# Agent attention and a SoLU layer on one core: the written-out order of five queues replaced by another

## The chip, the core and the metric

The kernel runs on one core of a Trainium2 chip. The metric is the device time of one execution in microseconds (us), as the median of several runs. Engines are called PE (TensorE matrix products; PEld its weight loads), DVE (VectorE), ACT (ScalarE), POOL (GpSimd) and SP (SyncE, which issues the DMAs here).

## What is computed

Four batches of 12,608 tokens with 128 channels, 49 agents per batch; the attention's output goes through a layer of 1,024 hidden units whose activation is a SoLU with a layer norm.

```python
a2k = sm(agents, k)                 # softmax(scale * agents @ k.T)
agent_v = a2k @ v
x = sm(q, agents) @ agent_v         # then reshaped to (50432, 128)
h = x @ w_in
solu = h * softmax(h)
ln = (solu - mean) / sqrt(var + 1e-06) * g_ln
out = ln @ w_out
```

## The kernel before

**Tiles.** The 50,432 tokens are 394 tiles of 128. All steps of all tiles are built as operations (class Op: an engine, a function, the operations it depends on) and issued in an order that a table gives.

**Phase A**, once per batch (`phase_a`, lines 562 to 825): 13 chunks of K and V come in by DMA (`kload` L580, `vload` L586 and L591), PE makes the agents' scores (L597), DVE their maxima, ACT the exponentials, PE turns them (L630) and multiplies with V (L650). At the end agent_v is multiplied with w_in, and the product stands in SBUF as two fp16 matrices, `mh` and `ml`. For batch 0 this is the head of the program; for the other batches it is spread over the tiles of the batch before.

**Phase B**, once per unit of 8 tiles (`phase_b`): queries come in by DMA (`qload` L840), PE makes logits (L858), DVE, ACT and POOL make exp and pack it as fp16 pairs (`pack`), a DMA transpose (L888) writes it turned to `pT` (a ring of 3), and PE sums it (L901) for the row's scale.

**Each tile x** then takes these steps:

- H (`c_h`, L950, PE): four products of 512 columns of pT with mh and ml into `ph`, a PSUM tile of 1,024 columns; there are two, `ph` of even and of odd tiles. H of x needs U of x-2.
- MX (`c_max`, L966, DVE): scaled copy of ph to `e` with its row extreme.
- EX (`c_exp`, L973, ACT): exp into ph, with its sum.
- U (`c_u`, L981, DVE): the product `u` (ring of 6), with its sum.
- SQ (`c_sq`, L1002, ACT): sum of squares.
- For 343 of the tiles: F0 (`c_f0`, L989 on POOL or L987 on ACT) rounds u to fp16 into `f` (ring of 5), F1 (`c_f1`, L992, POOL) writes the remainder beside it, XT (`c_x`, L996, SP) is a DMA transpose of both into `x` (ring of 8, x_a to x_h), and W (`c_w`, L1030, PE) multiplies it with w_out: 24 products of 128 columns, in four parts of six, between which other work may stand.
- For the other 51 tiles: PE turns u (`c_t`, L1009), ACT or DVE copies it (L1014), and W is 8 products in fp32.
- Four tiles share a PSUM tile `px` for their W. FIN (`c_fin`, L1077, DVE) scales the four by one over the standard deviation, and OUT (`c_out`, L1081) writes 256 KB to HBM. There are four `px`, which phases A and B use too.

**The order.** `STEPS` (lines 25 to 148) is a compressed table; `steps()` unpacks it to pairs of an operation's number and a choice of engine (F0, copies and small casts have two). `Plan.run` issues the operations in that order:

```python
        todo = steps()
        for i, k in todo:
            o = self.ops[i]
            e = o.eng[k]
            assert o.left == 0
```

So the table sets the order of instructions on each engine and of the transfers on SP's queue. Each engine works through its own in order and waits where data isn't there; no time of the plan is imposed. The model times that `Plan.run` keeps choose the `px` tile of an operation and the number of idle products that PE makes in the head (`idle`, L1088, of `ones`). At the end every instruction is tied to the one before on its engine, so nothing is moved later.

Of the kernel before, what the change touches and what calls it, by code (L numbers as in the profile page):

```python
# [25 lines left out]
    "c-pOb4^%5{THoX)aJejUZsTm6r7XQ7W%Fgz$cG#b%TkJIj44t?M8p`gk#Z0zMH;i&ER7tbkwaseBC<$Rj1kj_h=|C^i7}f^DN>}EL(^=&EagxR"  # L26
    "Vmii%91b6s8<Ls6Gm}3v3Ex@k>4lpxGw-~Ap7(ivzu)t`E&P)np-{NFVtSYm+VPdv>(=DZb?a7AaetXqY%4CuFE*FmC-MN0g_bwo+&A3%mBc2x"
    "Hy;`twfV+xSJiJ+ohYiPvCrHpeQU!F_jt$cy=i6L0PZ5X(-=BG|8`%P?5go-MplANg2jo3+x@wfNUdi3*tXHDn4UD&Yid>>CU&%7{ri6x>)<yz"
    "dNkG!+oR3_Y_r<X@!MYK$jWe|tG~v)bakMeHl4KZYp2IM?~dA0r+@aM_Z*#aAJs_1jnxUq*;Z5n0`h^CX_K&aK(q*eVJQuI{b>WfnXZ^1&V^`9"
    "2JlcF7LgxSV+m;lS2@~a0$Bp*ON2JPO|d(6EB2odW7sc!M@lOiM;H8?B5ec<Nh4qwiv%WzCsqe!n8FqTperdEys7(-A0!0}jTjal#(eS>XUrl)"  # L30
    "hvIe_7U(;|TmWb{?CAqR?51K8fBx=3LU-JD^w4YoldGaSbZfzl1JIqqcEu{pf!z;nv`X>KH&r(Zq19>-w}zsaI?-jG*dAZGz7_WzV?7vQiSic>"
    "8xd>GgBq77C2nw1s|jA1&>#4$W^Goq5%l4=qNwjoE5|KSp{u4g7@5{8eR}(YS+yC_@3qDcB;tBGoR%}Zgf@o<By0MxTc&l%T~nY!W2!+h;7Wwt"
    "YK!sb%R~L=b(q(^Xa(Zf7e4McYf>%fRsH?NUDMk$*ITtf|8`h>ej;pmBRIct=@UXJHneGMu4<Ct(M1%@{IB10X)I2(wMDxZl|=WFy)rB!jvbHU"
    "k%Now1Gh|SRLX!eD8;oBR4^`=Yxj1sj^iDp*0eKL)4bAsXSeLsb~G!5Nw8=&Y}M}Hm<WMn?1#VRJ?t7aMCKw<o9X)Ze>OVWxqOXvG>1XE9*Azy"
    "*jn<+^Cl(~yN4IsEgKz|jgEy4tPur^2jik!JUrLaCzCaA;$Dqtff)8n{7B_c)#a3FL8j{)Xl$vjBeoZ9P4z-Beh|}p0&=4Tbu?@Vc1<o!xY%SD"
    "4s1uJ6H(|asMgkWu)Xqg<Vp+=>9zaI+Of&5ElE_QyHii!;+}*-h@Ru!0Br6DQU^|DcmeQ<!xSzd<RAQ+S8HvSMWq{x?(Lz<Gh8MfTMx*$aP6>L"
    "@admkn=mzm8yy`xiTF<ZNIk+|f2z7@pI){atikkJLvQz}qfP2C&yGxt*Gj79=XPb55!-!Y$MD@>)_6{^w_~m2gFp2nmx7@I)B4!Oh*g3M>zpIb"
    "glG2=Pqw2V<s84PzUXYZu6c;mygf>YsvN4S`t9K;Mo6}YL(PH5nNhh47{o1p%-L6?{gp4CPtA01h0d(a!tJ3YM+8?WTJ9$CVPKxsRapGOu;iOR"
    "w=C7U7Y(+g1-E$m_hRC}*#fWy_k%J;C=dan(d!DAIB_eMeBp~D_>yKw?FB)Zd$^%<6djxs$A%-qsK+3Uw0ODz;M=C7H8WZ>4zR=)u2D4`-}pLi"
    "!Xw_E)4Iuh_h2P(0i^war~-ZaL(b~)p20u)8sYl$PmfpH$F&=ZISi`@V7dZWG;@FT0bx^0vFPc|ttHtX`tk3QYW%%ZE8r3{pEmF}WuByS_MiTN"  # L40
    "e|x&kuEr)--2F8b*KdKOeol%HpR^?FbV*a&PQ6{-9cZu*JXZI9^koaNG=;>5qjgTjMzc?UI5uN^`kn7-K!tkeLHCLhjr+rn4JAN?5tpIKv;fwH"
    "{K{G}I_l`DP!0Fb-^SJ9ctk05T4K>Bbr2IPrB-xeZ4>iYWkG#wNa?{1KKc1XP#BenV>45~_=QEK5fh^TDDH=K0q3I$2Gg0^QGwao=XzAT1H0$G"
    "sjWm;vrj!b;~5#+uJSe3R&CVzahc}vxV{|#tKlm@1GYyUqmFx(XXI}_99;(1*{g=f>bVt<X?6gw9Wgbcy93SPm3VJL1RRz%*{yid;Hs13?X4l("
    "{rn}~iGKK_Cw<cPKm6g?LAR{g9TSA7qwewESuw5y;H`OfV)4yA_@f_tux`YiOW*f3H&W-`@C6qi!RF<zRq51&@hhS9(pc}(AU@HyxaYnjaOSGA"
    "6E_PNhPVzGhhwV9&62NryDl9QsMI5v<eR^&@iyO1fqm_!%BI(-eKuD@ba1V41peOFu&Bu94frK$ARg$(lk2_c#*zRy1ARj4qNHchIqJCB(}!&C"
# [36 lines left out]
    "8pIPVap)D-fBLywv}(8Bv6RN{tA)3BPYr+l3(nx+&10e~Sknr+BifCi(5nYqO?6l2(nY00yfPIN2b?Yx%*q1dFRlINf!ZAi5lUj)Y*QQvh7Kmc"
# [1193 lines left out]
```

## Time and profile before

| | us |
|---|---|
| median of 3 runs (lowest, highest) | 1345.69 (1345.56, 1348.81) |
| the profiled execution, own time | 1351.38 |
| its span, first to last instruction | 1349.6 |
| mean granted TensorE clock | 0.980 |

How to read it: the rows further below come from one profiled execution. An engine's idle time stands beside the instruction that came after it, with what ended the wait. A DMA's row on SP is the time that SP took to issue it; its landing is told apart. Matmuls overlap, so the times of single rows on PE do not add up; the start of one to the start of the next does.

### The profile page before, as it was taken

How to read it: one execution, taken by the hardware profiler on the slowest of the kernel's cores; microseconds unless marked ns; L12 is line 12 of the kernel's file. 1: busy time of each engine (PE TensorE's matmuls, PEld its weight loads, DVE VectorE, ACT ScalarE, POOL GpSimd, SP SyncE). 2: the span in 40 equal slices, each digit the busy share in tenths (PEclk: the TensorE clock that was granted, in tenths of full speed). 3: DMA queues.
4: the chain of work that ended last, by engine and by line, in shares of the span. 5: the costliest groups of instructions: out<-in, count | busy, mean ns of one | idle time of the engine just before them, and what ended most of it. 6: DMA issues, size and time to landing. Idle time of an engine off the chain costs nothing.

```text
span 1349.6 us, 36468 instructions
## 1 busy us (share of the span) xinstructions
PE 1215.8 (90%) x14321; PEld 921.6 (68%) x14321; DVE 1179.0 (87%) x2124; ACT 1177.3 (87%) x2151; POOL 1133.5 (84%) x919
## 2 busy tenths in 40 slices
PE   8888898999998898988998888989999989999997
PEld 4666576777776676766767666766777767777676
DVE  6788797989998887988989888988899989999996
ACT  5579797988998987978989788988889989999997
POOL 3488697888997887887988889898789989999995
PEclk9899999999999999989999999999899999999999
DMA  9699999999999999999999999999998999999997
GB/s 375 181 211 221 240 214 245 234 234 185 216 235 232 231 237 229 201 241 225 216 210 216 220 240 228 246 239 244 227 192 177 231 216 211 213 208 224 193 194 176
DMA packets 805484, 300.62 MB, mean 223 GB/s; under 512 B 770496, under 2 KB 774080, under 8 KB 805312
## 3 DMA queue, kind: packets, MB, share of 16 engines
q1 hardware_dynamic: 805312, 298.30, 105.3%
q8 instruction: 112, 1.84, 0.6%
q14 instruction: 60, 0.49, 0.1%
HBM read 79.67 MB, written 25.82 MB: 78 GB/s over the span
## 4 chain that ended last, share of the span: by engine, by line
POOL 22%; DMA 19%; ACT 16%; PE 15%; issue 15%; DVE 12%; SPq 1%; POOLq 0%; DVEq 0%; ACTq 0%
ACT ph L973 7%; ACT sq L1002 6%; PE px L1030 6%; PE ph L950 4%; DVE e_b L966 3%; POOL f_a L992 3%; POOL f_d L992 3%; POOL f_b L992 2%; POOL f_e L992 2%; POOL f_c L992 2%; DVE e_a L966 2%; POOL f_e L989 2%; POOL f_b L989 1%; DMA x_a<-f_c 1%; POOL f_d L989 1%
## 5 line engine op out<-in xcount | busy, mean ns | idle before, releaser
L973 ACT ACTIVATE ph<-e_a,nm 128x1024 f32<-128x1024 f32 x197 | 219.0, 1112 | 74.6 <-DVE e_a L966 73.7
L973 ACT ACTIVATE ph<-e_b,nm 128x1024 f32<-128x1024 f32 x197 | 219.0, 1112 | 23.5 <-DVE e_b L966 22.4
L950 PE MATMUL ph<-mh,pT_a 128*128 128x512 f16 x264 | 101.5, 384 | 8.1 <-DVE u_a L981 4.4
L950 PE MATMUL ph<-mh,pT_b 128*128 128x512 f16 x260 | 99.4, 382 | 9.8 <-DVE u_c L981 3.7
L950 PE MATMUL ph<-mh,pT_c 128*128 128x512 f16 x260 | 99.7, 384 | 4.3 <-DVE u_a L981 1.2
L950 PE MATMUL ph<-ml,pT_a 128*128 128x512 f16 x264 | 101.5, 384 | 0.0
L950 PE MATMUL ph<-ml,pT_c 128*128 128x512 f16 x260 | 99.7, 384 | 0.0
L950 PE MATMUL ph<-ml,pT_b 128*128 128x512 f16 x260 | 99.2, 381 | 0.0
L1030 PE MATMUL px<-wh,x_f 128*128 128x128 f16 x688 | 75.6, 224 | 17.0 <-DMA x_f<-f_b 5.2
L966 DVE TENSOR_SCALAR_CACHE_REDUCE e_a<-ph,nk_a 128x1024 f32<-128x1024 f32 x49 | 62.6, 1278 | 29.4 <-PE ph L950 29.0
L1030 PE MATMUL px<-wh,x_g 128*128 128x128 f16 x688 | 75.2, 225 | 13.6 <-DMA x_g<-f_d 4.3
L981 DVE SCALAR_TENSOR_TENSOR u_a<-e_a,cb,ph 128x1024 f32<-128x1024 f32 x66 | 84.1, 1275 | 3.4 <-ACT ph L973 2.5
L1030 PEld LDWEIGHTS <-x_f 128*128 128x128 f16 x1032 | 65.5, 101 | 31.0 <-DMA x_f<-f_b 6.0
L981 DVE SCALAR_TENSOR_TENSOR u_d<-e_b,cb,ph 128x1024 f32<-128x1024 f32 x66 | 84.2, 1276 | 2.1 <-ACT ph L973 1.5
L981 DVE SCALAR_TENSOR_TENSOR u_c<-e_a,cb,ph 128x1024 f32<-128x1024 f32 x65 | 82.9, 1276 | 3.2 <-ACT ph L973 2.6
L981 DVE SCALAR_TENSOR_TENSOR u_b<-e_b,cb,ph 128x1024 f32<-128x1024 f32 x65 | 82.9, 1275 | 2.4 <-ACT ph L973 2.2
L981 DVE SCALAR_TENSOR_TENSOR u_e<-e_a,cb,ph 128x1024 f32<-128x1024 f32 x65 | 82.9, 1275 | 2.0 <-ACT ph L973 1.5
L981 DVE SCALAR_TENSOR_TENSOR u_f<-e_b,cb,ph 128x1024 f32<-128x1024 f32 x65 | 82.9, 1276 | 1.6 <-ACT ph L973 1.1
L1030 PEld LDWEIGHTS <-x_g 128*128 128x128 f16 x1032 | 65.2, 101 | 27.6 <-DMA x_g<-f_e 5.6
L1030 PE MATMUL px<-wh,x_d 128*128 128x128 f16 x688 | 73.4, 221 | 10.9 <-DMA x_d<-f_e 4.4
L950 PEld LDWEIGHTS <-pT_b 128*128 128x128 f16 x520 | 47.1, 98 | 50.3 <-issue 20.9
L1030 PE MATMUL px<-wh,x_b 128*128 128x128 f16 x688 | 73.5, 221 | 7.3 <-DMA x_b<-f_e 3.7
(473 smaller groups left out, 4811.2 us busy)
## 6 DMA issues: line engine op xcount, KB each, us to landing
out_dram<-ob_a SPq DMA_DIRECT2D x49, 256.0 KB, 3.6
out_dram<-ob_b SPq DMA_DIRECT2D x49, 256.0 KB, 2.8
qt_a<-in_qT_dram SPq DMA_DIRECT2D x24, 512.0 KB, 4.7
qt_b<-in_qT_dram SPq DMA_DIRECT2D x24, 512.0 KB, 4.8
kt_a<-in_kT_dram SPq DMA_DIRECT2D x18, 512.0 KB, 5.0
kt_b<-in_kT_dram SPq DMA_DIRECT2D x18, 512.0 KB, 5.1
vt_b<-in_v_dram SPq DMA_DIRECT2D x18, 512.0 KB, 5.1
vt_a<-in_v_dram SPq DMA_DIRECT2D x18, 512.0 KB, 5.0
```

What stands on the lines that cost most here:

```text
L950: nc.tensor.matmul(ph[:, sl], w, m[:, sl], start=(q == 0), stop=(q == len(mm) - 1))
L966: nc.vector.tensor_scalar(out=nhs[x], in0=phs[x], scalar1=nkr[k % 4][:, j : j + 1], scalar2=None, op0=ALU.mult, op1=ALU.min, accum_out=nms[x])
L973: nc.scalar.activation(out=phs[x], in_=nhs[x], func=AF.Exp, scale=-1.0, bias=nms[x], accum_out=rs_[R]["S"][:, j : j + 1])
L981: nc.vector.scalar_tensor_tensor(out=u, in0=nhs[x], scalar=scal(x)[:, 4:5], in1=phs[x], op0=ALU.mult, op1=ALU.mult, accum_out=su)
L989: nc.gpsimd.tensor_scalar(out=f[:, 0, :], in0=us[x][0], scalar1=1.0, scalar2=0.0, op0=ALU.mult, op1=ALU.add)
L992: nc.gpsimd.tensor_tensor(out=fs[x][:, 1, :], in0=us[x][0], in1=fs[x][:, 0, :], op=ALU.subtract)
L1002: nc.scalar.activation(out=sq, in_=u, func=AF.Square, bias=su, scale=-float(DF), accum_out=rs_[R]["Q"][:, j : j + 1])
L1030: nc.tensor.matmul(po, ut, wt[:, kf, :], start=(q == 0), stop=(q == len(mm) - 1))
```

## The change

`STEPS` holds other numbers, and the table is one line longer, so that every line behind it counts one more (L1030 is now L1031). No other line differs: the same 6,893 operations, tiles, ring sizes and transfers, and the same code. The order was planned anew, with a reserve between the landing of each transfer and the use of its data; the planner is not part of the file.

```diff
 STEPS = (
-    "c-pOb4^%5{THoX)aJejUZsTm6r7XQ7W%Fgz$cG#b%TkJIj44t?M8p`gk#Z0zMH;i&ER7tbkwaseBC<$Rj1kj_h=|C^i7}f^DN>}EL(^=&EagxR"
...
+    "c-pOb4^V1tdf(v{y<9%y7<$T_&vmS^#!!|J<G99J$8}xGu!dU48p2xE5Mmi)EaMu+5^AlnhOmTK;~K|WYKbw_u+|u3T-UI~_!&d2>l%jevDO%C"
...
 )
```

The same place on PE in both orders, the second-layer product of tile 135, whose transposed data stand in x_g (x_f is tile 134, t_b tile 136; ph_167 is H of an odd tile, ph_166 of an even one). Before:

```order
L950 MATMUL ph_167<-mh_4346,pT_a 128x512
...
L1009 MATMUL px_169<-ident,u_e 128x128 x4
L1030 MATMUL px_171<-wh_93,x_f 128x128
...
L1030 MATMUL px_171<-wh_93,x_g 128x128
...
L858 MATMUL px_169<-ag_sb,qt_a 64x49 x16
L1030 MATMUL px_168<-w_92,t_b 128x128 x2
L950 MATMUL ph_166<-mh_4346,pT_a 128x512
```

The first row is H of tile 141, the last H of tile 142. Now:

```order
L951 MATMUL ph_166<-mh_4319,pT_a 128x512
...
L631 MATMUL px_169<-ident,ek_b 128x128 x4
...
L951 MATMUL ph_167<-mh_4319,pT_a 128x512
...
L1031 MATMUL px_170<-wh_93,x_g 128x128
...
L651 MATMUL px_169<-vt_a,eT_a 64x128 x8
...
L1031 MATMUL px_168<-w_92,t_b 128x128 x6
```

Here the first rows are H of tile 142 and the first half of H of 143: the first product of tile 135 stood behind H of 141 and stands now behind H of 142 and half of 143. Over all 343 transposed tiles, the last tile whose H has begun ahead of W of tile x is x + 6.5 in the mean before and x + 7.3 now; x + 5 or less for 49 of them before and for 8 now.

The queue of SP around the transpose of tile 135 (x_g<-f_d), before:

```order
L996 DMA_TRANSPOSE x_e<-f_b 128x16x128
L996 DMA_TRANSPOSE x_f<-f_c 128x16x128
L586 DMA vt_b<-in_v_dram 128x1024
L840 DMA qt_b<-in_qT_dram 128x1024
L1081 DMA out_dram<-ob_a 128x512
L996 DMA_TRANSPOSE x_g<-f_d 128x16x128
L888 DMA_TRANSPOSE pT_c<-pack_a 128x8x128
L1081 DMA out_dram<-ob_b 128x512
L580 DMA kt_a<-in_kT_dram 128x1024
L996 DMA_TRANSPOSE x_h<-f_e 128x16x128
```

Now:

```order
L997 DMA_TRANSPOSE x_e<-f_b 128x16x128
L581 DMA kt_a<-in_kT_dram 128x1024
L841 DMA qt_b<-in_qT_dram 128x1024
L997 DMA_TRANSPOSE x_f<-f_c 128x16x128
L1082 DMA out_dram<-ob_b 128x512
L1082 DMA out_dram<-ob_a 128x512
L997 DMA_TRANSPOSE x_g<-f_d 128x16x128
L581 DMA kt_b<-in_kT_dram 128x1024
L587 DMA vt_b<-in_v_dram 128x1024
L889 DMA_TRANSPOSE pT_c<-pack_a 128x8x128
L997 DMA_TRANSPOSE x_h<-f_e 128x16x128
```

Before, two loads and a store stand ahead of x_g; now two loads stand ahead of x_f and two stores ahead of x_g. Over the queue from its 60th transfer on, a load of K, V or Q stands directly behind another one 29 times before and 48 times now, and three in a row 6 times before and 13 now.

PE's end, from the last H (ph_167 of tile 393) on. Before:

```order
L950 MATMUL ph_167<-mh_13491,pT_a 128x512
...
L1030 MATMUL px_168<-wh_93,x_e 128x128
...
L1009 MATMUL px_170<-ident,u_c 128x128 x4
L1009 MATMUL px_171<-ident,u_c 128x128 x4
```

Now:

```order
L951 MATMUL ph_167<-mh_13536,pT_a 128x512
...
L1031 MATMUL px_168<-wh_93,x_c 128x128
...
L1031 MATMUL px_171<-wh_93,x_d 128x128
...
L1031 MATMUL px_171<-wh_93,x_e 128x128
...
L1010 MATMUL px_170<-ident,u_c 128x128 x4
```

Between the last H and the turn of tile 392 (u_c) stood the W of x_d from its middle and that of x_e and part of x_f; now a quarter of x_b, and the W of x_c, x_d and x_e, which is 1.75 tiles' W more behind the last H in all.

## Rows read from the trace of the kernel before

**Rows 1.** Page, part 1: busy time, share of the span, instructions of each engine.

```profile
PE 1215.8 (90%) x14321; PEld 921.6 (68%) x14321; DVE 1179.0 (87%) x2124; ACT 1177.3 (87%) x2151; POOL 1133.5 (84%) x919
```

**Rows 2.** Waits: who <- for whom: us in total, times, longest.

```profile
ACT ph L973 <- DVE e_a L966: 73.7, 63, 6.9
DVE e_a L966 <- PE ph L950: 59.0, 44, 6.3
```

**Rows 3.** Line L996, the transposes: who waited (us, times); time from issue to landing.

```profile
  PE px L1030: 72.3, 63
...
DMA to landing us min/median/max: 3.6/4.6/9.9
```

**Rows 4.** Timeline of SP near 520 us: start, time to issue, line, transfer.

```profile
519.99 0.54 SPq L586 DMA_DIRECT2D vt_b<-in_v_dram  x1
520.59 0.45 SPq L840 DMA_DIRECT2D qt_b<-in_qT_dram  x1
...
521.63 5.57 SPq L996 DMA_TRANSPOSE x_g<-f_d  x1
527.62 1.26 SPq L888 DMA_TRANSPOSE pT_c<-pack_a  x1
```

**Rows 5.** Timeline of PE there: start, us; in brackets the idle time before.

```profile
531.59 0.29 PE L1030 MATMUL px<-wh,x_g 128*128 128x128 f16 x1 [4.32 <-DMA x_g<-f_d]
```

**Rows 6.** Who waited for L996 in six windows from 100, 400, 500, 600, 800 and 900 us (us, times).

```profile
  PE px L1030: 10.0, 10
  PE px L1030: 11.4, 10
  PE px L1030: 11.0, 6
  PE px L1030: 1.0, 1
  PE px L1030: 4.8, 5
  PE px L1030: 2.9, 4
```

**Rows 7.** The six windows: length, busy us (instructions) by engine, PEclk, DMA share, GB/s.

```profile
100.00:200.00 100.00, 87.54 (x1031) 64.19 (x1029) 85.93 (x152) 85.55 (x157) 80.35 (x63) 1.00 1.16 227
400.00:500.00 100.00, 89.68 (x1040) 67.04 (x1039) 86.71 (x151) 87.40 (x162) 83.52 (x66) 0.98 1.11 236
500.00:600.00 100.00, 88.85 (x1001) 67.48 (x1000) 82.54 (x146) 83.48 (x155) 79.38 (x63) 0.95 1.09 225
600.00:700.00 100.00, 91.86 (x1137) 71.58 (x1136) 88.32 (x164) 89.49 (x168) 85.59 (x69) 0.98 1.10 223
800.00:900.00 100.00, 91.84 (x1106) 69.06 (x1104) 90.11 (x162) 89.80 (x166) 87.22 (x65) 1.00 1.13 236
900.00:1000.00 100.00, 88.16 (x1050) 67.76 (x1048) 85.20 (x155) 86.24 (x163) 84.81 (x68) 0.97 1.13 237
```

**Rows 8.** Waits of PE: four pairs of tiles with their longest wait last.

```profile
PE px L1030 <- DMA x_a<-f_c: 5.7, 3, 4.0
...
PE px L1030 <- DMA x_b<-f_e: 3.7, 1, 3.7
...
PE px L1030 <- DMA x_f<-f_a: 4.7, 3, 3.3
...
PE px L1030 <- DMA x_f<-f_b: 5.2, 3, 3.2
```

**Rows 9.** Waits of PE for the transposes of phase B, same columns.

```profile
PE px L901 <- DMA pT_c<-pack_a: 3.6, 2, 2.1
PE px L901 <- DMA pT_b<-pack_b: 2.4, 1, 2.4
```

**Rows 10.** Timeline of weight loads near 521 us: the W of one tile, 24 loads.

```profile
521.03 1.44 PEld L1030 LDWEIGHTS <-x_e 128*128 128x128 f16 x24
```

**Rows 11.** Timeline of PE near the end: the turn of tile 392.

```profile
1337.04 1.09 PE L1009 MATMUL px<-ident,u_c 128*128 128x128 f32 x8 [0.36 <-DVE u_c L981]
```

More of the change, by code (lines that the diff above doesn't have):

```diff
@@ L31 @@
[L31 to L45, printed above, removed]
@@ L146 @@
[L146 to L147 removed]
+    "c-pOb4^V1tdf(v{y<9%y7<$T_&vmS^#!!|J<G99J$8}xGu!dU48p2xE5Mmi)EaMu+5^AlnhOmTK;~K|WYKbw_u+|u3T-UI~_!&d2>l%jevDO%C"
+    "tb3NB)VcL?y@==ZJ%7M+z}@a-diBbm^ZtF_=lT79&+|5%HlcBS<ffq`UgsKbl!B@gAO*^#f9z;y=|r-w(s*v?TL*7$^~r!bQh5T@hW@6iG52--"
+    "onL*H(C;bhOk3T{8@-bC-I@7uP<|X7R);Q|uFCFkd8{QQPt;28E<jz`dCS#)#j(29slGKPJ=kQg`|eoNcrhz3*Eq&^ug30obu;AyjlDHDV`}we"
@@ new lines @@
+    "YVlrKVKW-<BBFTWYVxG1eD&H=hF+CT*LO*F5@)jssbr^2Au*`BB?kR@C!qj+wl@-ouiuSD6(Fd(wM_VjD*))(EXj0l35A-PdBfTle`AQaLzBv&"
+    "JR#rxq3_6(@}rDYf^9b|*4xmCFl3)GV2-YB`>+0N<fJPwf^Vdf&a+*U+}xwK-qabSs1)d$`V+g>8GwR%6!V2{|HF?YQKe+@)Pt=_o%RZRb!7%s"
+    "B?AgPvJ2V=60J8EZT`fz$-AeSQO$h#)5lj%G<bVHZSsz{-}?4YxWFD%_l2LF10zned`jA*?$HG{o8*0-^78|qD-3!LfVD(s+yTQWr?GZ^`3w*Z"
+    "jm{ZI60D4f49m%#2(}EDqnR;uXikS0g7f#78*7OguS>_`D%=H(86UnX0p$ad@rZYqs0!f|*M6n16^%59_a?T~yBZZb-ZrP~O|FgN34K(tDC^iO"
+    "zgDi*D&5<=ohI*Uh01Hyt-CAHaJ(a`Jhqp4zWr4bs`3v7V<4TX(Q7T2p_PC%3glkX&;3erWqa=0dw}bWE5?;zTpp3{y2U$-y$YW`)*I`(=-LiM"
@@ new lines @@
+    "mcS4H)fzt9-qN1L9p{>z-oahJW9#^~Ryh`PtoCdg&XvjA=DE0|b9Z{;ZrPOFGI^&49I4?+h4|hzj9p@pW}`N!s@%5WO@m8d?qK81zCsf10+(1|"
+    "Y3;nRRWj?fY4^`mD>AGaG}U{4^F#3KzotEwfW7$SB}QPW6ke+x-#Kd<U26~H$`f-P_~_e?(<(eY=EKmKucHHK_8K47@W`}1yi<J*H`0P`f92m9"
+    "tv!eHmL}rV)!zn&7BdbV-qEQVw-NfmYBymDjWzeiq@vQpo3k;E-V{*Sw$O{ZgLZ%#2HV!p^kC?JkS={x8k1Xmhw{LdT|bBZ+Hcezw%MK58Tp2K"
+    "#aKFF?>$@|xU)OUZ>zQSj)C!tDTlXj(BJJV)g9XJB*RjjTvq{R!HD+o&1@hvF>Nc?*GwMB?<>dg<>~dorOv9YMgO-x)q6ZIRhV{h`L$SebgC%r"
+    "@n6+UG%jzYu(Q2jP!^~<nO`6}Ce$Kx<KTTl4v3@_Pn?;+&6%<qq;x*Rl7A)^x0o72RlP`M9P<f>H^W1C^lWM7&LG?G*f}4Kq8q(4<*swg{bQe%"
@@ new lines @@
+    "Oj~dnK<5JqFTUbg0}Ya2{<1sXC0{sJjp5S4$UYiUl%30ff2cYDErN|{<7fJS8ueSE*k1457X^nqb#EfAmA0>Z6vOt00Q?ukG!K&ag4L<}+_(2M"
+    "Da*RYbkck)mV$%k+k@)%w2!bXL>CrB>5MUL-oPfo@Pd6pJd_qKDNl!8|LYgVmBZfpQ(K~9V58-5Y^(&7znM?m>lPL<Apk?Nkx)nfENXtRjaLjR"
+    "S4a2jwVP7ilEgAlwbhN@RHa3-^MCPsfB2!k-zdT2LCa<1p}5gJSPe2rEHa#wnY*>|tukfBimLL`*K{_Lkj28{ChTkfFfFt9`A37Q)be<&q8y+T"
+    "oh<`~3fWl$x~@Brc$$@p8I9Cy`p<vq?P@nt&H+3&7%xpd;+u+5XLDQzR`Au?Giz7{WampW4Kv=YDU011wT*ap4$oA3s<nDWxKfpB3B^_&vormx"
+    "p*u<Y!mxHHT<fSGAasZ4sfrS?8gpD$40%!DP3YFm^Z)1Xnmr?P130d6bjwonolVzM3!=#>%^o2=Zob;tU*B4&@*F7=O&6>34?bCQa@I$fyTx6X"
@@ new lines @@
+    "m{E4Nt@GkdU>i4st&46nB6ry%n=O5WBe8gmiB6h)h7wf|s>F2RgZ5b6;V_8!>f3EDsn*#Zlh0dB>8(u_Ix+olq*`dx>>Q27#j<smx9Z|h5BEN^"
+    "w|C`l^iRY;^^M(;3f&N9{ki{UK!kWZIBSSTPL}<8FgiP`MWaNbO|_qtJI7AvkLOi*2SBI9O?U!7mac+*NdTy#`U$DKcD8es7y=KD>9sy-OXzZI"
+    "RP#%pv0d+lP_TZmV>4sZ_A(gyj&p49y88MG$9sU~cmHheZZ2>*5#8{ot}x<{KWuyuUrw%~ojvBxg_@&QO=Ef)gu)#@{mjzu|MJ;gTyHc+&&IE6"
+    "jv|9VtL_{fa~oIMOVkqZ@qe0;FUfZunn2iUT&b5@!%kp|-bYubXJ;+i#e<lt!>0P^3zJ1;%~UX;*aelssnN3v_hMUAw>C0*HWZaeW9QhIyZNFt"
+    "1;DZH{ytHo4#XNHKym=emKMQUM=Axx)#K(1Me|i{uswu{kMV9Gy@bbNUXGZYO6`ugBUEbe>7A}cd1!FW2Ar}`*LG*yQEAm;aD!O1xit66YLD4-"
@@ new lines @@
+    "8eE{FNzQ^uvM>`RkvxLr%Ygh8i=Q6m0We3^Aq6@G;TLE5>qGdWltlQFv7op`=GQI?3sMEAUyxAp-K)^4`Lc!ND$PQUCi#HP&khUr!^und$i}4$"
+    "k`Jf|KV2qYKr)2PzwF|t3p}>Uzx3dSKz`wjOTN77EYBAF;qua(ml!lJTgqZCg5;H#3aTi45=D>~5~93)@VSeZ_vO`UNrYFu{eCaIxGs>(K9Ir;"
+    "ERQt!F3aBvHvs>imt9;9f#gelGB02H+g^6@%4^RF4_SE2k|!IH{9@emxFkO}=dYK)7rss^OcwaZ#1m-T<P~|rPx-ijyj;pfxXBU^pt+^>eB|Nf"
+    "2Zet3GBqLvVym#Q$}0hWx63XhkLdDJ_3!Jl3n2?Hy9#!gAL9kehJV?GynNY(<flu#%dVFau)>w_6Wjvm;iqMJmt7oSK@e_jI4}Fn!*nta(|IQ3"
+    "+V=ar>_YO!EWGS05Rv(pUC8&i>_W)zdfA1LFO-eG$7L4}j{a7cUF84g%dY<mXk@!;"
```

201 lines of the change are left out of this document (95 added, 106 removed).

## The prediction

> **What bounds the kernel now.** I read the shares of the engines first: PE is busy for 1215.8 of 1349.6 us, DVE, ACT and POOL for 1133 to 1179 [rows 1]. No engine is full, and none is much idler than the others, so time is lost in waits between engines that are all needed. The waits come next. ACT waits for DVE's MX, and DVE's MX waits for PE's H [rows 2]: 73.7 us and 59.0 us for the even tiles alone. So H is late, and what makes PE late is to be looked for on PE. The line of the transposes tells it: PE waited 72.3 us in 63 places, just ahead of a W, for a transpose to land; the landing takes 4.6 us from the issue in the median, 9.9 us at worst [rows 3]. That is over half of PE's 133.8 us of idle time (1349.6 - 1215.8).
>
> One place shows how. SP issues a load, another load and a store, and then the transpose x_g at 521.63 us; that issue alone takes 5.57 us, and the next row begins at 527.62 [rows 4]. PE comes to W of that tile and stands idle for 4.32 us until 531.59, when x_g lands, 9.9 us after its issue [rows 5]. PE works in order, so the next H stands behind this W, and behind that H stand MX, EX and U.
>
> What a microsecond of such waiting costs is read from six windows of 100 us. Three have 10.0, 11.4 and 11.0 us of it, three 1.0, 4.8 and 2.9 [rows 6]. DVE, whose busy time I take as the pace, is busy for 85.93, 86.71 and 82.54 us in the first three, mean 85.1, and for 88.32, 90.11 and 85.20 in the others, mean 87.9 [rows 7]. So 7.9 us less waiting (10.8 against 2.9) go with 2.8 us more work done: 0.36 us per us. The pairs scatter (82.54 against 88.32 gives 0.58, 86.71 against 85.20 less than nothing), so the factor is an estimate between 0 and 0.7.
>
> **The change part by part.** No operation, tile or transfer is added or removed; all of it is order.
>
> *W later on PE.* W of a transposed tile stands behind 0.8 tiles' H more than before. At 1349.6 / 394 = 3.4 us per tile that is 2.7 us at most; I take 2.5 us more between landing and use. The mean wait is 72.3 / 63 = 1.15 us [rows 3]. The five longest I find are 4.32 [rows 5], 4.0, 3.7, 3.3 and 3.2 us [rows 8]; beyond 2.5 us they keep 1.8, 1.5, 1.2, 0.8 and 0.7, in all 6 us. So some 66 us of PE's waiting go if landings stay where they are: 66 x 0.36 = 24 us. What hides nothing here is W itself: it is the same work with an older tile's data, so PE always has as much to do between two H as before. H goes on waiting only for U of two tiles back, and that pair isn't moved. FIN on DVE waits for W; counted in the order, it moves by 0.6 tiles too (11.8 tiles behind the MX of its last tile instead of 11.2), and a px tile is held from its first W to FIN for 7.6 tiles both times, so I cost both at nothing. If FIN were not late enough, DVE would stop there with U behind it.
>
> *The sums of phase B (L901)* wait 3.6 and 2.4 us for their transposes [rows 9]; they too stand a tile later (8.9 behind the transpose instead of 7.9). 6 x 0.36 = 2 us.
>
> *Transfers closer together.* SP's queue now has three loads in a row 13 times instead of 6. A transpose behind such a cluster lands like x_g, after 9.9 instead of 4.6 us [rows 3 to 5], 5.3 us late, of which the reserve takes 2.5. Seven places x 2.8 = 20 us of new waiting on PE, x 0.36 = 7 us lost. The ends: nothing, if the loads cost the same wherever they stand, and 19 more pairs of loads x 2.8 x 0.36 = 19 us.
>
> *The end.* Everything deferred must be done at last: 1.75 tiles' W stand more behind the last H, at 1.44 us for 24 weight loads [rows 10], 2.5 us. Before, PE waited only 0.36 us for DVE there [rows 11], so nothing covers it. *The head* moves the same bytes and is left at nothing; bounds of 3 us either way, since its loads are reordered.
>
> The sum: -24 - 2 + 7 + 2.5 = -16.5 us. The profiled execution took 1351.4 us itself, 5.7 more than the median of 1345.7; 1351.4 - 16.5 = 1334.9 there, and **1329 us** as a median.
>
> **A rule that speaks against it.** On SP the rows near 520 us stand end to end: each issue begins where the one before ended, give or take 0.4 us [rows 4], and the 16 DMA engines are at a share of 1.09 to 1.16 in all six windows [rows 7]. The Trainium skill (Perfetto Trace Analysis, "What 'DMA-bound' means") calls a kernel DMA-bound where the issuing engine's track is solid DMA slices; an order that uses the data later lands nothing sooner, and by that rule alone the sum would be 0. The trace agrees for such stretches. Against it: the window of 600 to 700 us has the same DMA share as 500 to 600 (1.10 and 1.09), 10 us less waiting on PE, and 5.8 us more work on DVE [rows 6, 7]; so the queue leaves room.
>
> **The rivals.**
>
> *A. The queue sets the pace* (what the rule above would do here). If transfers come at the rate SP and the DMA engines give, a W moved later finds no earlier landing: the wait shrinks on PE and comes back on POOL, which needs `f` buffers that land late, and on SP. For it: the solid rows and the share above 1. Against it: the pair of windows just named. Time: 1345.7 plus the 2.5 us of the end, 1348 us at most; no change that can be told.
>
> *B. Slower: the clusters.* The mechanism sits in SP's queue: 48 pairs of adjacent loads instead of 29. If each of the 19 new ones makes the transpose behind it land as late as x_g, PE gets 19 x 2.8 = 53 us of new waits, 19 us of time; and as transposes are issued in the order of tiles, the ones behind are late as well, so that half of the gain goes (24 falls to 12). Time: 1345.7 - 12 + 19 + 2.5 = 1355 us. It decides from the point where landings behind clusters come over 2.5 us later than now, beyond the reserve. For it: the x_g place. Against it: two adjacent loads need not take more of the queue in all than two apart.
>
> *C. The change doesn't do what it says*, since the planner's reserve is met only in its own model. The order speaks against it for W (5 tiles or fewer of distance for 8 tiles instead of 49); for the loads of K and V there is nothing of it to be seen, the mean distance is 11.2 tiles both times. Its time would be that of A, and it is counted there.
>
> **How the numbers follow.** A measurement of this kernel tells 0.3% from no change, 4 us. My forecast, W's waits gone and the pace up, gets 0.62; A with C 0.15; B, with whatever else a new order of five queues does worse, 0.23. Faster is then 0.62, same 0.15, slower 0.23. The low end: a factor of 0.7 instead of 0.36 on 72 us is 50 us, less 2.5 of the end: 1298; taken as 1300. The high end takes in A and B's 1355, as 1356; about 1 in 10 is left out on each side.
>
> **What would show it.** In the new profile: the wait of PE for L996's transposes falls from 72.3 us to under 25, while the landing time stays near 4.6 us in the median; DVE's MX waits less for H; PE's busy share rises above 91%. B would show in a median landing above 5.5 us and in waits of PE that stay above 50 us; A in short waits of PE beside longer ones of POOL for u or f, and an unchanged time. Wrong altogether would be the prediction if PE's waits vanish, landings stay and the time doesn't fall: then the pace is set by the ring of MX, EX and U alone, and the factor of 0.36 was chance.

## The result, and the profile after

The changed kernel takes 1302.5 us (median of four runs, 1298.3 to 1307.2) where the kernel before, timed beside it on the same chip, takes 1347.3: a ratio of 0.966, 95% interval 0.962 to 0.971, so 45 us less. The forecast was 17 us less. Its sign and its range held; its size came out at well under half of what was measured.

The page of the changed kernel, part 1, against [rows 1]:

```profile
PE 1204.2 (93%) x14305; PEld 916.7 (71%) x14305; DVE 1177.5 (91%) x2127; ACT 1174.8 (90%) x2157; POOL 1131.2 (87%) x910
```

Busy times hardly move (DVE 1179.0 to 1177.5; PE 1215.8 to 1204.2, at a mean granted clock of 0.985 for 0.980); the span falls from 1349.6 to 1299.0 us, so nearly all of the gain is idle time. Its waits (who <- for whom: us in total, times, longest) against [rows 2]:

```profile
ACT ph L974 <- DVE e_a L967: 28.9, 32, 5.5
DVE e_a L967 <- PE ph L951: 27.2, 32, 6.0
```

73.7 and 59.0 us have become 28.9 and 27.2: H comes in time more often. The line of the transposes (who waited; issue to landing) against [rows 3]:

```profile
  PE px L1031: 26.2, 30
...
DMA to landing us min/median/max: 3.6/4.7/11.2
```

PE's wait for W's data fell from 72.3 us in 63 places to 26.2 in 30 while the landing stayed (4.6, now 4.7 us). I had asked for under 25 us and an unchanged landing as the sign that the main step was right; it came to within 1.2 us of that. What I had not expected stands in the queue of SP (start, us to issue, line, transfer). First the kernel before:

```profile
608.32 1.75 SPq L996 DMA_TRANSPOSE x_b<-f_c  x1
610.12 0.58 SPq L580 DMA_DIRECT2D kt_a<-in_kT_dram  x1
610.79 2.06 SPq L996 DMA_TRANSPOSE x_c<-f_d  x1
612.90 0.58 SPq L586 DMA_DIRECT2D vt_b<-in_v_dram  x1
613.58 4.00 SPq L996 DMA_TRANSPOSE x_d<-f_e  x1
617.68 0.53 SPq L586 DMA_DIRECT2D vt_a<-in_v_dram  x1
618.30 6.11 SPq L996 DMA_TRANSPOSE x_e<-f_a  x1
624.51 1.58 SPq L996 DMA_TRANSPOSE x_f<-f_b  x1
```

Then the changed kernel:

```profile
597.71 2.42 SPq L997 DMA_TRANSPOSE x_g<-f_c  x1
600.22 0.53 SPq L841 DMA_DIRECT2D qt_b<-in_qT_dram  x1
600.80 0.42 SPq L841 DMA_DIRECT2D qt_a<-in_qT_dram  x1
601.32 0.38 SPq L587 DMA_DIRECT2D vt_b<-in_v_dram  x1
601.79 7.33 SPq L997 DMA_TRANSPOSE x_h<-f_d  x1
609.22 2.25 SPq L997 DMA_TRANSPOSE x_a<-f_e  x1
611.57 1.69 SPq L997 DMA_TRANSPOSE x_b<-f_a  x1
```

Before, three loads, each alone between transposes, take the queue from 610.12 to 624.41 us with the three transposes behind them, 14.3 us. After, three loads together take 600.22 to 609.12 with one transpose; two more, at 2.25 and 1.69, make about 13.0. The load itself is issued in 0.4 to 0.6 us. Its price shows in the issue of the transposes behind it. It need not be the next one: the 0.58 us of kt_a are followed by an issue of 2.06 us, the next load by 4.00, the third by 6.11. These long issues are no waits for POOL: for each of the 395 transposes of the kernel before, the tile that it reads was finished before its issue began.

The same over the whole queue: I take the time from the end of one transpose's issue to the end of the next one's, where the next one is of a tile, no store stands between the two and SP did not idle. In the kernel before its mean is 2.35 us with nothing between (165 places), 4.66 with one load (33) and 6.54 with two (6). The 17 traces in which all loads are issued give 2.36 us (2653 places), 4.74 (425), 6.49 (137) and, with three loads, 6.82 (33). So the first load costs 2.4 us, the second beside it 1.75, the third 0.3.

To add this up I take from the trace the **time in flight**: the time during which at least one packet of any transfer is under way. It is 1278 us before and 1245 after, for the same bytes. So 34 of the 51 us by which the span fell are time in flight. A second sum used below is the time that engines waited for landings of any transfer: 122 us before, 84 after.

### The profile page after: what moved, and what is told of

The parts are those of the page before. It is cut to its first block, busy times and chain, and to the rows that moved or that the text cites. A ratio compares the mean times of both kernels' runs of the same rounds, so it can differ in the third digit from the quotient of the medians.

```text
span 1299.0 us, 36435 instructions
## 1 busy us (share of the span) xinstructions
PE 1204.2 (93%) x14305; PEld 916.7 (71%) x14305; DVE 1177.5 (91%) x2127; ACT 1174.8 (90%) x2157; POOL 1131.2 (87%) x910
## 4 chain that ended last, share of the span: by engine, by line
ACT 30%; DMA 16%; PE 15%; POOL 13%; DVE 13%; issue 12%; SPq 1%; DVEq 0%; POOLq 0%; ACTq 0%
ACT ph L974 13%; ACT sq L1003 12%; PE px L1031 6%; PE ph L951 4%; DVE e_b L967 2%; POOL f_c L993 2%; POOL f_b L993 2%; DVE e_a L967 2%; POOL f_e L993 2%; DMA x_f<-f_d 2%; PE px L651 2%; DMA out_dram<-ob_a 1%; POOL f_a L993 1%; POOL f_d L993 1%; DVE u_a L982 1%
## 5 line engine op out<-in xcount | busy, mean ns | idle before, releaser
L974 ACT ACTIVATE ph<-e_a,nm 128x1024 f32<-128x1024 f32 x197 | 218.6, 1109 | 30.1 <-DVE e_a L967 28.9
L982 DVE SCALAR_TENSOR_TENSOR u_a<-e_a,cb,ph 128x1024 f32<-128x1024 f32 x66 | 84.2, 1276 | 5.4 <-ACT ph L974 4.4
L982 DVE SCALAR_TENSOR_TENSOR u_d<-e_b,cb,ph 128x1024 f32<-128x1024 f32 x66 | 84.2, 1276 | 2.5 <-ACT ph L974 2.1
L951 PEld LDWEIGHTS <-pT_a 128*128 128x128 f16 x528 | 47.9, 99 | 48.3 <-issue 21.1
L951 PEld LDWEIGHTS <-pT_c 128*128 128x128 f16 x520 | 46.8, 98 | 46.2 <-issue 17.6
L1031 PE MATMUL px<-wh,x_f 128*128 128x128 f16 x688 | 73.0, 221 | 5.1 <-DMA x_f<-f_d 2.2
L1031 PEld LDWEIGHTS <-x_a 128*128 128x128 f16 x1032 | 64.0, 99 | 18.9 <-DMA x_a<-f_b 3.4
L1031 PE MATMUL px<-wh,x_a 128*128 128x128 f16 x688 | 73.4, 221 | 4.0 <-DMA x_a<-f_b 2.4
L1031 PEld LDWEIGHTS <-x_f 128*128 128x128 f16 x1032 | 63.9, 99 | 18.1 <-DMA x_f<-f_d 2.4
L1031 PE MATMUL px<-wh,x_e 128*128 128x128 f16 x688 | 72.5, 219 | 3.9 <-DMA x_e<-f_c 1.3
```

What stands on the lines that cost most here:

```text
L951: nc.tensor.matmul(ph[:, sl], w, m[:, sl], start=(q == 0), stop=(q == len(mm) - 1))
L974: nc.scalar.activation(out=phs[x], in_=nhs[x], func=AF.Exp, scale=-1.0, bias=nms[x], accum_out=rs_[R]["S"][:, j : j + 1])
L982: nc.vector.scalar_tensor_tensor(out=u, in0=nhs[x], scalar=scal(x)[:, 4:5], in1=phs[x], op0=ALU.mult, op1=ALU.mult, accum_out=su)
L1031: nc.tensor.matmul(po, ut, wt[:, kf, :], start=(q == 0), stop=(q == len(mm) - 1))
```

## The experiments

Every kernel was timed against the kernel before on the same chip, except the one of the queue by itself. Chips differ by some 10 us in the time of the kernel before, so ratios are compared. Where the order is edited, only numbers of `STEPS` change; the edit is told in words, and rows of the queue show a place of it.

### Is it the place of W?

Four kernels move W alone along PE's order, with FIN and the stores behind it, by whole parts of a tile's turn.

**W one tile later in the order of before.**

Each part of W (a fourth of a tile's, for transposed tiles) goes where the fourth part behind it stood. The same place of PE's order in both:

```diff
-L1030 MATMUL px3_171<-wh16_93,x_e_116 128x128
+L1025 MATMUL px1_169<-wh16_93,x_d_115 128x128
```

> The order of before, with every W on PE moved four parts (one tile) later, and FIN and OUT moved along; the other operations of DVE, ACT, POOL and SP keep their order. Theory 1, W's place on PE is what gained and a us of PE waiting for a transpose costs about one us: waits of PE for L996 fall from 72 to 20-30 us, time 1295-1315 us. Rival 2, W's place gives only the 0.36 us per us of the prediction and the rest of the 45 us comes from the new orders of the other queues: same fall of the waits, time 1325-1335 us.

Measured: 1372 us, ratio 1.014 (1.010 to 1.019). PE's wait for the transposes fell to 8.8 us, yet the kernel is slower. DVE waits less for H than before, but PE now waits for DVE, and DVE for stores:

```profile
ACT ph L968 <- DVE e_a L961: 51.5, 54, 3.4
...
DVE e_a L961 <- PE ph L945: 36.9, 46, 3.1
...
DVE ob_a L1072 <- DMA out_dram<-ob_a: 25.5, 10, 5.8
PE ph L945 <- DVE u_c L976: 19.8, 14, 5.4
...
PE px L1004 <- DVE ob_b L1072: 10.2, 7, 2.8
```

Over all buffers PE waits 48.9 us for U (21.2 before) and 34.6 us for a FIN that frees a px buffer (9.9 before); DVE waits 27.8 us for stores (16.5 before). So a W that comes later holds its px buffer longer. The shift also changed who hands px buffers to whom (by the kernel's own plan, 169 of the 492 operations that take one take it over from another operation than before), so the kernel doesn't test the reserve of W cleanly. It does show that PE's wait for W's data can go almost entirely and leave the time no shorter.

**W half a tile earlier in the order of before.** Here each part goes where the second part ahead of it stood; the edit is the same otherwise.

> The order of before with every W half a tile (two parts) earlier, to read the price of a wait on the other side. Theory 1: waits of PE for L996 rise from 72 to 100-120 us and the time by as much, 1375-1395 us. Rival 2 (0.36 us per us): 1355-1365 us.

Measured: 1402 us, ratio 1.036 (1.029 to 1.043), PE's wait 107.1 us in 66 places.

**W one tile earlier, and one tile later, in the changed order.** Each part goes where the fourth part ahead of it stood, or the fourth behind it.

> The order of the change, with every W on PE moved one tile earlier (FIN and OUT along), so that the reserve is taken back while all else of the new order stays. Theory 1: waits of PE for L996 rise from 26 to 70-90 us and the time goes back to 1340-1360 us. Rival 2: the waits rise as much, but the time only to 1315-1325 us.

> The order of the change with every W one tile later still. Theory 1 taken alone: the 26 us of waits fall under 10 us and the time to 1280-1290 us. If the ring of MX, EX and U sets the pace by now, or the rings of x and px fill: 1298-1310 us, with waits of PE for U (L951) up. Rival 2: 1295-1300 us.

Measured: 1377 us, ratio 1.018 (1.012 to 1.023), with 48.8 us of PE's wait; and 1333 us, ratio 0.986 (0.982 to 0.990), with hardly any. Moved either way, W makes the changed order slower, by 5% and by 2% of the time before. With W later, PE waits 41.1 us for a FIN that frees a px buffer, where the changed kernel has 1.8. All four times lie outside the ranges expected. So these four kernels change more than W's reserve. For that alone the order has to stay and the data has to change.

**Same order, older data.** W reads the transposed data of the tile before, which landed a tile's turn sooner, so its products are of other tiles. Each x buffer is then held a tile longer; SP's own wait for W is 3.5 us in this kernel (1.4 before).

```diff
-po, t = st[G]["po"][:, j * P : (j + 1) * P], pr[x]
+po, t = st[G]["po"][:, j * P : (j + 1) * P], pr[fl[max(fl.index(x) - 1, 0)] if xbar(x) else x]
```

> The order of before, untouched on all five queues; W of a transposed tile reads the transposed data of the tile before it in place of its own (each product has the same shape, but the second layer is computed on the neighbouring tile's hidden values). So the data have a whole tile more to land and no instruction moves. Theory 1, the waits of PE for the transposes cost about a us of time per us: waits of PE for L996 fall from 72 to under 10 us, time 1280-1305 us. Rival 2 (0.36 us per us, the rest of the change's gain being other order): 1320-1332 us. Rival 3, the place of W doesn't matter at all without the new order (as the shifted orders seem to say): 1340-1350 us.

> The order of the change with the same substitution. Theory 1: the 26 us of waits left fall under 5 us and the time from 1302 to 1278-1290 us. Rival 2: 1292-1298 us. Rival 3: 1300-1305 us.

Measured: in the order of before 1344 us, ratio 0.995 (0.992 to 0.998), 6 us gained; in the changed order 1296 us, 0.962 (0.955 to 0.968), which can't be told from the change (0.966). PE's wait for W's data fell from 72.3 to 20.0 us, and the gain is a tenth of that. The wait went to the next use. The waiters of line L888, the transposes of phase B, before:

```profile
  PEld L901: 10.0, 9
  PE px L901: 7.3, 5
```

With W relieved:

```profile
  PEld L901: 35.9, 18
  PE px L901: 31.5, 14
```

DVE's wait for stores and POOL's for f rose too, from 16.5 to 30.5 us and from 14.8 to 36.3. All waits on landings together went from 122 up to 147 us. So W's reserve alone is worth 6 us and not the 24 of the forecast.

### Is it the place of the loads?

**Loads brought together, and loads pulled apart, by delaying some.** In the first, in the order of before, a load waits for the next one if that is near; in the second, in the changed order, the second of two neighbours goes behind the next transpose.

The first has 46 pairs of neighbours for 23, the second 7 for 41. (Neighbours are counted here in steps of the plan, as in the expectations. A short step issues several transfers, so the figures are smaller than those of the section on the change, which counts transfers.) A place in the queue of the first:

```diff
-L586 DMA vt_b<-in_v_dram 128x1024
 L1081 DMA out_dram<-ob_a 128x512
 L996 DMA_TRANSPOSE x_d<-f_e 128x16x128
 L996 DMA_TRANSPOSE x_e<-f_a 128x16x128
+L586 DMA vt_b<-in_v_dram 128x1024
 L840 DMA qt_b<-in_qT_dram 128x1024
```

> The order of before with loads of K, V and Q on SP moved later to stand directly ahead of the next load (46 adjacent pairs instead of 23, counted by load steps; the change has 41). Rival 4, the clusters themselves help, since loads and transposes mix less on the DMA engines: 1325-1340 us. Theory 1: no gain, 1345-1360 us, with longer landings behind clusters and waits of PE for L996 at 72 us or more.

> The order of the change with adjacent loads pulled apart (7 pairs instead of 41): the second load goes behind the next transpose. Rival 4: slower, 1315-1330 us. Theory 1: within 8 us of the change's 1302 us, as long as waits of PE for L996 stay near 26 us.

Measured: 1355 us, ratio 1.004 (1.001 to 1.006); and 1320 us, 0.978 (0.973 to 0.983), which is 16 us lost of the 45. The time in flight moved with the neighbours, though by 8 us only in the first: 1270 us for 1278, and 1270 for 1245 in the second. Both delay loads, though, so that K and V come later: PE's waits for them rose from 10.5 to 24 us in the first and from 10 to 30 in the second. So the 16 us can't be given to the queue alone.

**Only the loads change places.** Each load goes behind the transpose behind which the other kernel has it; everything else keeps its order. (Which px buffer an operation takes follows the model times, and so shifts a little: 18 of the 492 operations that take one, and 8 in the counterpart, take it over from another operation.) A piece of SP's queue early in the program, for the order of before with the loads of the change; the counterpart is made the same way.

```diff
 L996 DMA_TRANSPOSE x_a<-f_a 128x16x128
+L840 DMA qt_b<-in_qT_dram 128x1024
+L586 DMA vt_b<-in_v_dram 128x1024
 L580 DMA kt_a<-in_kT_dram 128x1024
 L580 DMA kt_b<-in_kT_dram 128x1024
 L996 DMA_TRANSPOSE x_b<-f_b 128x16x128
 L888 DMA_TRANSPOSE pT_c<-pack_a 128x8x128
 L996 DMA_TRANSPOSE x_c<-f_c 128x16x128
-L840 DMA qt_b<-in_qT_dram 128x1024
 L996 DMA_TRANSPOSE x_d<-f_d 128x16x128
```

> The order of before on all engines, its transposes and stores too; only the loads of K, V and Q stand elsewhere in SP's queue: behind the same transpose as in the changed order (112 of 125 placed loads move, 45 pairs stand together instead of 23). Theory 1 (loads that stand together cost the queue less, and that is most of the gain): 1310 to 1328 us, the time with a transfer in flight down by 20 us or more. Theory 2 (the reserve ahead of every use of a transfer is the gain, the place of the loads is incidental): 1338 to 1352 us, with PE's wait for transposes near 70 us. Theory 3 (both, and they hold only together): no gain or a loss here, 1345 to 1375 us.

> The counterpart: the changed order, with the loads of K, V and Q behind the transposes where before has them (24 pairs together instead of 41). Theory 1: it loses most of the gain, 1325 to 1345 us, with 20 us more time with a transfer in flight. Theory 2: 1298 to 1312 us. Theory 3: a loss of about half, 1315 to 1330 us, with waits of PE for K or V.

Measured: 1350.6 us, ratio 1.002 (0.999 to 1.006); and 1343.0 us, 0.993 (0.989 to 0.996). So the loads' new places alone are worth nothing, the rest of the changed order alone 10 us, and both together 45. The first is what theory 3 said. The second lost more than the half that theory 3 gave it, and its time lies in the range of theory 1. The time in flight did follow the loads, 1252 us in the first (26 less than before) and 1276 in the second (31 more than the changed kernel). But in the order of before the shorter queue was not used. Line L888's waiters in before_loads:

```profile
  PEld L901: 28.7, 9
  PE px L901: 25.2, 8
```

A place that has no reserve takes what a long row of loads costs at one moment (7.3 us before, 25.2 now), and all waits on landings stand at 132 us, 10 more than before.

### Is the queue the bound at all?

```diff
         def vload(c):
...
+            if b > 0: return
```

> Before, without the 36 full and 9 short loads of V of the second to fourth batch; the products with V read what the buffers hold, so the output is not the reference's. Orders of all engines are untouched and every engine does the same work; only the transfer queue has some 36 x 2.2 = 79 us less to do. Theory 1 (the queue is nearly the bound): 1345 falls by 45 to 80 us, to 1265 to 1300, all of it ahead of 980 us, where these loads stand. Theory 2 (late uses stall engines that work in order, but the queue's total is not the bound): the waits fall a little, as transposes land sooner, and the time by 10 to 30 us, 1315 to 1335.

> The same loads left out of the changed order (output not the reference's for the same reason). Theory 1: 1302 falls by 30 to 60 us, and stands within 15 us of before without these loads, as the place of loads matters less with fewer of them. Theory 2: it falls by under 15 us, as there is little waiting left, and the distance to before without these loads stays over 20 us.

Measured: 1288.5 us, ratio 0.952 (0.944 to 0.960), and 1251.2 us, 0.926 (0.920 to 0.933). With the order unchanged, 36 full loads less (and 9 short ones) save 61 us by the medians, 1.7 us for each full one at most; by the ratios it is 65 us, and 54 in the changed order. Of the time in flight 77 and 58 us went, so the span follows it at about 0.8 and 0.85 us per us (59 of 77, 50 of 58). The queue is near the bound in both kernels. Two smaller things go with it: PE's 6 us of waits for V, and 13 us of PE's busy time (1215.8 to 1202.3), at a mean granted clock of 0.990 for 0.980. The distance between the two kernels stays 37 us, where theory 1 had under 15: they differ by more than the place of these loads.

### Reserve at every use, without moving anything

Two of the uses that wait can be given more buffers: seven of f for five, four of ob for two. They are taken from the ring of t, which keeps five of its eight. For the other two, W and the sums of phase B (L901), older data is read: of the tile before, and of the unit before.

```diff
-    obr = ring(2, [P, GT, P], F32, "ob")
+    obr = ring(2, [P, GT, P], F32, "ob") + [tr[5][:, 4 * i : 4 * i + 4, :] for i in range(2)]; fx = fr_ + [t.rearrange("p f t -> p (f t)").bitcast(F16).rearrange("p (a f) -> p a f", a=2) for t in tr[6:]]
-        f = fs[x] = fr_[fl.index(x) % FBUF]
+        f = fs[x] = fx[fl.index(x) % 7] if x >= 40 else fr_[fl.index(x) % FBUF]
-            obs[G] = obr[G % 2]
+            obs[G] = obr[G % 4] if G >= 10 else obr[G % 2]
-            pr[x] = tr[tl.index(x) % TBUF]
+            pr[x] = tr[tl.index(x) % 5]
```

and for the kernels with "reserve" in their name, beside the line of W above:

```diff
-                nc.tensor.matmul(px[:, j : j + 1], ptr[k % PTB][:, j, :], ones16, start=True, stop=True)
+                nc.tensor.matmul(px[:, j : j + 1], ptr[(k - (k > 7)) % PTB][:, j, :], ones16, start=True, stop=True)
```

**The buffers alone, in the order of before.**

> The same buffers in the order of before. Waits of POOL for f (15 us) and of DVE for ob (16.5 us) go. Joint theory (a shorter queue and reserve at every use are both needed): under 8 us gained, 1338 to 1348, as PE's wait for W's transposes stays at 65 to 75 us. If the reserve at f and ob is what the changed order has ahead, 1315 to 1335.

Measured: 1355.6 us, ratio 0.999 (0.996 to 1.001). POOL's and DVE's waits went (14.8 to 2.4, 16.5 to 0) and PE's for W rose from 72.3 to 84.2: again one wait for another.

**All four uses, with the loads of before and with those of the changed order.**

> Order and loads of before, with reserve at all the uses that were seen to wait: 7 f and 4 ob buffers, W reads the transposed data of the tile before, and the sums of phase B (L901) those of the unit before (output not the reference's). Joint theory: the queue keeps its time with a transfer in flight (1278 us), and nothing can stand far under that plus some 50 us: 1325 to 1338. If reserve alone is the gain: 1295 to 1315. If neither, because H, MX, EX and U are ordered badly: 1340 to 1348.

> As the one before it, with the loads at the places of the changed order (order of all engines still that of before; output not the reference's). Joint theory: the queue's time falls to some 1250 us and the uses have their reserve, so that the time comes near that of the changed kernel: 1298 to 1315, 20 us or more under the kernel with the loads of before. If reserve alone is the gain: within 6 us of the one before it. If neither: 1340 to 1350.

Measured: 1333.5 us, ratio 0.983 (0.979 to 0.988), and 1308.0 us, 0.963 (0.959 to 0.966). Reserve at all four uses gains 23 us with the loads of before; with the loads moved too it gains 51, as much as the change, though every other operation keeps the order of before. The time in flight is 1286 and 1252 us. The waits on K in the two (PE, L597):

```profile
PE px L597 <- DMA kt_b<-in_kT_dram: 18.3, 4, 7.6
...
PE px L597 <- DMA kt_a<-in_kT_dram: 2.8, 3, 1.1
```

in the first, and in the second

```profile
PE px L597 <- DMA kt_a<-in_kT_dram: 8.8, 3, 5.6
...
PE px L597 <- DMA kt_b<-in_kT_dram: 1.0, 2, 0.7
```

So the new places of the loads bring K sooner as well, by 11 us of PE's waiting (21.1 for 9.8), beside the shorter queue. V comes sooner too: PE's waits for it are 11.3 and 4.9 us.

**The fourth cell: changed order, loads of before, reserve.**

> The fourth cell: the changed order on all engines, the loads at the places of before, and the reserve by buffers and older data of loads_reserve (output not the reference's). If the rest of the changed order is worth only the reserve that it holds: near before_reserve, a ratio of 0.975 to 0.988. If its order of H, MX, EX and U is better by itself: a ratio of 0.95 to 0.967, as with the loads at their new places. The time with a transfer in flight stays near 1276 us in the first case.

Measured: 1339.4 us, ratio 0.986 (0.983 to 0.990), time in flight 1290 us. It stands with before_reserve (0.983). With the loads of before, the order of H, MX, EX and U in the change is worth nothing by itself. With the loads of the change that is not shown: there the changed order with the added buffers has 0.956 (further below), loads_reserve 0.963.

The ratios in one table:

| order of the rest | reserve added | loads of before | loads of the change |
|---|---|---|---|
| before | no | 1 | 1.002 |
| before | yes | 0.983 | 0.963 |
| change | no | 0.993 | 0.966 |
| change | yes | 0.986 | 0.956 (buffers alone), 0.962 (W's older data alone) |

The time in flight goes by the columns and not by the rows. With the loads of before it is 1276 to 1290 us in six kernels (before, w_prev, before_rings, before_reserve and the two of the changed order), with those of the change 1245 to 1252 us in five, whatever the reserve and the time.

**The buffers in the changed order.**

> The changed order untouched, with 7 buffers of f in place of 5 and 4 of ob in place of 2 (from tile 40 on; the added ones lie in t buffers that are free after the head), so that POOL waits for no transpose and DVE for no store; all data as in the reference. If what is left in the changed kernel is lateness at these two places (21 and 14 us), 1302 falls by 5 to 15 us, to 1287 to 1297. If the queue's time alone is left, under 4 us.

Measured: 1298.5 us, ratio 0.956 (0.952 to 0.959). The changed kernel had 0.966 (0.962 to 0.971). The two intervals don't touch, but the two kernels were not timed beside each other. By the ratios it is some 14 us better than the change. Its span is only 4 us under that of the change (1295.2 for 1299.0), on another chip, so what a direct comparison would show stays open.

### What a load costs by its neighbours

Nothing computes here: SP issues transfers of the kernel's sizes in rows and mixtures, the f tile being the source of every transpose.

```diff
...
+    for i in range(48):
+        nc.sync.dma_start_transpose(**X())
+    for i in range(48):
+        nc.sync.dma_start(**L())
+    for i in range(48):
+        nc.sync.dma_start_transpose(**X())
+        nc.sync.dma_start(**L())
...
```

Behind these stand the same two by two, four by four, and with two transposes to a load, then the stores.

> The queue by itself: no engine computes anything (the output is zeros), SP issues transposes of one f tile and loads of 512 KB, the sizes of this kernel: 48 transposes in a row, 48 loads in a row, then both in turn one by one, two by two, four by four, and two transposes to one load; then the stores. Theory (a load between transposes costs more than one beside another load): one by one, a transpose and a load take 4.5 us or more together; four by four at least 0.5 us per pair less; the sum of a transpose and a load from the rows of one kind is 0.5 us or more under one by one. Rival (a load costs the same wherever it stands, and the shorter time in flight of the changed order comes from idle time that fell away): all three mixtures within 0.2 us per pair of the sum from the rows of one kind.

Measured, by line (durations of one issue in ns, min/median/max, then the first and last start in us): transposes in a row (L371), loads one by one (L376), two by two (L381), four by four (L386), one behind two transposes (L390).

```profile
L371 SPq DMA_TRANSPOSE x<-f x48: 1847/2409/3277, 3.0 to 120.4; - x48
L376 SPq DMA_DIRECT2D k<-in_kT_dram x48: 569/574/575, 184.8 to 389.9; - x48
L381 SPq DMA_DIRECT2D k<-in_kT_dram x48: 427/507/1193, 396.4 to 592.2; - x48
L386 SPq DMA_DIRECT2D k<-in_kT_dram x48: 328/430/947, 604.8 to 780.8; - x48
L390 SPq DMA_DIRECT2D k<-in_kT_dram x24: 579/970/1187, 790.2 to 947.8; - x24
```

A transpose in a row takes (120.4 - 3.0) / 47 = 2.50 us. A transpose and a load one by one take (389.9 - 184.8) / 47 = 4.36; two by two, with one issue of 0.6 us off the end, (195.8 - 0.6) / 23 / 2 = 4.24 per pair; four by four, less 1.6, (176.0 - 1.6) / 11 / 4 = 3.96. Behind two transposes a load costs 157.6 / 23 - 5.00 = 1.85. In a row of their own, 46 loads (two had gone at the start) were issued between 122.4 us and 176.1, 1.17 us each; their landings, from 127.0 to 185.0 us, are 1.29 us apart, and that is the price to take, since the queue filled: a load landed 4.7 us after its issue at the start of the row and 10.2 us at its end. So a load costs 1.9 us where it stands alone, 1.3 in a row, and 3.79 would be the sum of the rows of one kind, 0.57 less than one by one. The rival, one price wherever it stands, falls. Two sizes of the theory were too large, though: one by one 4.36 and not 4.5, the gain of four by four 0.40 and not 0.5 per pair.

By these prices the change, with some 34 lone loads fewer, would shorten the queue by some two fifths of the measured 34 us: a load in fours costs (4 x 3.96 - 4 x 2.50) / 4 = 1.46 us, 0.4 less than a lone one, and 34 x 0.4 = 14. By the spacings inside the kernels it is most of it: from the 60th transfer on, before has 66 places with one load between transposes, 22 with two and 13 loads in larger groups; after has 31, 22 and 48. At 2.4 us, 4.1 us for two and about 1.5 per load of a larger group ((6.82 - 2.36) / 3) that gives 268 and 237 us, 31 less. Why a lone load costs 2.4 us among the other work and 1.85 by itself was not settled.

## Why the prediction was right in sign and wrong in size

**W later on PE (-24).** What it said of the trace came true: 72.3 fell to 26.2 us, the landing stayed, MX waits less, PE is at 93%. What it said of the price did not: relieving W alone takes 52 us of waiting away and is worth 6 us (w_prev), 0.12 us per us and not 0.36, as L901, f and ob wait in its place. Reserve at all four uses is worth 23 us. That this is almost the number I gave to one of them is luck: the factor of 0.36 [rows 6, 7] did not price W's waits. The waits for landings of all transfers are as long in the three windows with little waiting for W (12.7, 8.9 and 15.8 us) as in the other three (12.3, 10.0 and 11.6), and over all twelve windows from 100 to 1300 us DVE's busy time falls by 0.9 us per us of them. In the new kernel the same six windows have 89.7 us of DVE in the mean, for 86.5 before.

**The sums of phase B, L901 (-2).** The wait is 5.7 us for 7.3, no gain to speak of by itself; but they are the use to which the wait moves when W is relieved alone (31.5 us), so their reserve is part of what makes W's worth anything.

**Transfers closer together (+7): this is the step that failed.** It took x_g's landing behind two loads and a store [rows 3 to 5] as the price of a cluster, and multiplied it by the new clusters. Those 5.3 us are about what the queue spends on two neighbouring loads and a store in any case (4.1 us the loads); the step counted the lateness of one transpose and not the total of the queue. That total falls when loads stand together: the time in flight is 34 us shorter. With reserve at the uses the new places of the loads gain 28 us (0.983 to 0.963; 51 less 23), and in the changed order itself 36 (0.993 to 0.966); the earlier K and V are a part of both that was not separated. A term entered as a loss of 7 was a gain of 28 or more. With 23 for the reserve, that is 51 us, which is what loads_reserve gained, and 6 more than the change.

**The end (+2.5)** cost next to nothing: from the last product of H to the end it is 16.3 us before (1349.6 - 1333.3) and 16.6 after (1299.0 - 1282.4).

**FIN and px**, left at nothing, did cost nothing in the change: PE's wait for a FIN that frees px fell from 9.9 to 1.8 us. With W a tile later and the rest unchanged it is 34.6.

**Rival A**, the queue as the pace, was closer to the truth than its chance: 36 loads less save 61 us. Its conclusion was wrong all the same. It held that an order can land nothing sooner at a given rate, and the rate is itself set by the order. By the Trainium skill (Perfetto Trace Analysis, "What 'DMA-bound' means") a solid track of the issuing engine marks one kind of such a kernel. The trace agrees only in part: the issues fill 1119 of 1349.6 us of SP's track before and 1113 of 1299.0 after. The share tells nothing of the order, though: 83% with more lone loads, 86% with clusters, which have 34 us less time in flight.

**Rival B** named the right place, loads that make the transpose behind them late, and does decide where there is no reserve: before_loads has it, 26 us less time in flight and not a microsecond gained. The sentence that I had put against it ("two adjacent loads need not take more of the queue in all than two apart") was the one to follow further: they take less.

**What stays open.** The split of the 28 us between a shorter queue and earlier loads; the part of a lone load's price in the kernels (2.4 us) that the queue by itself (1.85) doesn't show; and why a load's price falls beside another load, which no run shows. That none of the edits tried reproduces the change alone is shown by the table; that an order with W moved alone suffers from px buffers held longer was read from its waits and not tried apart.

## What to carry to other kernels

Count what a queue of transfers takes in all before counting who is late: put loads together, as a pair of a transpose and a load took 4.36 us one by one and 3.96 four by four here, and give every use behind such a group its reserve, since a reserve at one use alone handed most of the wait to the next. A factor read from windows prices all that varies between them; before it is given to one wait, ask what the others did. And to test one cause in a written-out order, leave the order and change the data or the buffers: four of four kernels that moved W along PE's order were slower than what they started from.

## What was not expected of the hardware

The price of a load depends on its neighbours and shows in the issue of the transposes behind it: 1.75 us without a load ahead, 2.06, 4.00 and 6.11 with one each, 7.33 with three. With nothing but the loads' places different, the issues of all 395 transposes take 983 and 947 us (order of before, loads of before and of the change), 1022 and 972 (the same with reserve), 1000 and 983 (changed order). By itself, a load of 512 KB costs the queue 1.85 us alone between transposes and 1.29 us in a row of loads. And the median landing told nothing of all this: 4.6 us before, 4.7 after, 4.4 in before_loads and 5.1 in before_reserve, which is 23 us faster than the kernel before.
